# A fused attention and two-layer MLP kernel on one Trainium2 core: the first batch goes through layer 1 in single precision, and the inverse sums of the last two batches are spread by DMA

## The chip, the core and the metric

The kernel runs on one core of one Trainium2 chip. The core's engines are TensorE (PE in the profile; its weight loads are PEld), VectorE (DVE), ScalarE (ACT), GpSimd (POOL), and SyncE (SP), whose queue issues all the DMA transfers of this kernel. The metric is the device time in microseconds of one launch.

## The reference

Four batches of eight heads with 576 queries and keys of 64 features go through an attention whose scores are cut at a threshold under the row maximum. The result, 2304 rows of 512 features, goes through two MLPs with a hidden width of 2048.

```python
scores = (1 / sqrt(64)) * q @ k.T
thresh = max(scores, -1) - tau
scores = where(scores >= thresh, scores, -1e9)
attn = exp(scores - max(scores, -1));  attn = attn / (sum(attn, -1) + 1e-9)
x = (attn @ v) laid out as (2304, 512)
h = x @ w_in;   x = (s * maximum(h, 0) ** 2 + b) @ w_out           # layer 1
h = x @ w2_in;  out = (h / (1 + exp(-1.702 * h))) @ w2_out         # layer 2
```

## The kernel before

**Attention.** The heads are taken as 16 pairs, four to a batch. A pair has nine tiles of 128 queries: four of the first head, four of the second, and a ninth with the last 64 queries of both. A tile (tile_step, L425) is: scores on TensorE (L447; plain single precision, two halves of the array at once), row maximum on VectorE (nm, L456), two small VectorE instructions, exp on ScalarE (e, L474), threshold and row sum on VectorE (L478), a float16 copy on ScalarE and its rest on GpSimd (p, L487 and L488), and a DMA that transposes both (L490) into PT0, PT1 or, for the ninth tile, PTm. When a pair's nine tiles are through, finish_sums (L492) forms the inverse row sums ri. They are needed along the free axis of rs and rm; TensorE transposes a broadcast of ri (eight transposes at L525 and one at L529) and ScalarE copies the four results out. finish_main (L542) multiplies with V (mix, 28 matmuls at L550) and scales by rs in x (L561); finish_last does the same for the ninth tile from PTm (L585). Batches 0 and 1 keep x in SBUF (tiles xa and xb); batches 2 and 3 store it to DRAM (xd) and load it later.

**MLP.** Of layer 1 and layer 2, hidden (L714) makes a 128-wide slice of the hidden units from four slices of the input (L723), and project (L753) multiplies four such slices with the output weights (L779). Each operand is split in a rounded high part and the rest (split, L650; copy at L321 on VectorE or L325 on ScalarE; subtraction at L340 on VectorE or GpSimd), and each product takes three matmuls in the faster mode for 32-bit data: xa with wh, xa low with wh, xa with wl. Weights are first converted (convert, L654: three VectorE instructions at L676, L680 and L687, three ScalarE and one GpSimd, L697) and stored in DRAM (wd); for the first use they are split straight from that result (ww), later they are loaded again (wl from wd).

**Order.** All steps are put in a list and a planner (Plan.run, L120) makes the order of every engine's instructions when the program is built, from priorities (the table KN, whose t0 to t4 are due times of the passes) and costs. Each engine then executes its list in order. The passes are: layer 1 of batch 0, layer 1 of batch 1, layer 2 of both, layer 1 of batch 2, layer 1 of batch 3 with the 64-row remainders of all batches, and layer 2 of these. Attention of the next batches is woven into the passes.

Of the kernel before, what the change touches and what calls it, by code (L numbers as in the profile page):

```python
# [280 lines left out]
class Kernel:  # L281
# [9 lines left out]
    def consts(self, pool):  # L291
# [3 lines left out]
        self.identr = pool.tile([P, P], F32R, name="identr")  # L295
        nc.scalar.activation(self.identr, self.ident, AF.Copy)
# [67 lines left out]
    def prep_qk(self, p):  # L364


        nc, add = self.nc, self.plan.add
        b, hp = p["b"], p["hp"]
        k = self.at("k", [P, 2, HALF], F32, bufs=2)
        q = self.at("q", [P, 2, S], F32, bufs=2)  # L370
        p["qk"] = k, q
        self.load(lambda: k.ap, lambda: self.k[b, hp], [k], P * S * 4)
        self.load(lambda: q.ap, lambda: self.q[b, hp], [q], P * 2 * S * 4)
        add(
            {"ACT": act(S) + 93.0},
            lambda _: nc.scalar.activation(k.ap, k.ap, AF.Copy, scale=self.qs), [k], [k],
        )

    def prep_v(self, p):
# [6 lines left out]
        mx = self.at("mx", [P, 2], F32R)  # L386
# [11 lines left out]
        def spread(_):  # L398
            for h in range(2):
                nc.tensor.transpose(T[:, h].bitcast(F32R), mx[:, h : h + 1].to_broadcast([P, P]), self.identr)  # L400
# [24 lines left out]
    def tile_step(self, p, i):  # L425
# [3 lines left out]
        k, q = p["qk"]  # L429
        Sp = self.ps("S", [P, 2, 512])  # L430
        if i < 8:
            h, t = divmod(i, 4)
            PT, part = p["PT"][h], t
            cols = slice(t * P, (t + 1) * P)
            pt = lambda: PT[:, :, cols]
            heads = [(h, slice(0, P))]
        else:
            PT, part = p["PTm"], None
            cols = slice(MAIN, S)
            pt = lambda: PT.ap  # L440
            heads = [(0, slice(0, H2)), (1, slice(H2, P))]

        def scores(_):
            for h, to in heads:
                for half in range(2):
                    r = slice(half * H2, (half + 1) * H2)
                    nc.tensor.matmul(Sp[to, half, :HALF], q[r, h, cols], k[r, h, :])  # L447

        add({"PE": (pe(1, HALF, True) + 200.0, 60.0)}, scores, [k, q], [Sp])
# [42 lines left out]
    def finish_sums(self, p):  # L492
# [9 lines left out]
        if p["early"]:  # L502
# [39 lines left out]
    def finish_main(self, p):  # L542
# [16 lines left out]
        add(  # L559
            {"DVE": dve(512) + 61},  # L560
            lambda _: nc.vector.scalar_tensor_tensor(x.ap, Up.ap, vcol.ap, rs.ap, ALU.mult, ALU.mult), [Up, vcol, rs], [x],  # L561
        )
        blk, hp = self.stay.get(p["b"]), p["hp"]
        if blk:
            if "x" not in blk:
                blk["x"] = self.xtile(blk)
# [34 lines left out]
    def attention(self, pairs):  # L601
# [3 lines left out]
        for n, p in enumerate(pairs):  # L605
# [11 lines left out]
            for i in range(R):  # L617
# [7 lines left out]
                if i in (0, 4):  # L625
                    p["PT"][i // 4] = self.at(
                        "PT%d" % (i // 4), [P, R, MAIN], F16, KN["pt%d" % (i // 4)],
                        (self.xp, "xb", 1) if i else None,
# [4 lines left out]
                if i == R - 1:  # L633
                    p["PTm"] = self.at("PTm", [P, R, P], F16)
                do(lambda p: self.tile_step(p, i), p, i)
# [4 lines left out]
    def heads(self, b, start, pace, lend=False):  # L640
# [3 lines left out]
                "early": b * NP + hp < KN["early"],  # L644
# [9 lines left out]
    def convert(self, m, f, which):  # L654
# [8 lines left out]
        w, wi = lambda: wb[:, :512], lambda: wb[:, :512].bitcast(I32)  # L663
# [5 lines left out]
        def size(_):  # L669
# [20 lines left out]
            [wa, (st, 1)], [wb],  # L690
# [6 lines left out]
        add({"POOL": pool(512)}, lambda _: nc.gpsimd.tensor_tensor(wi(), wi(), low(), ALU.add), [(st, 0), wb], [wb])  # L697
        self.load(lambda: wd[:, f, :], w, [(wd, f)], P * 2048, reads=[wb])
        return wb
# [14 lines left out]
    def hidden(self, m, w, x, n):  # L714
# [4 lines left out]
        terms = [(w[i], j, kk) for kk in range(KD) for i, j in ((0, 0), (0, 1), (1, 0))]  # L719

        def mm(_, part):
            for i, (wt, j, kk) in list(enumerate(terms))[part]:
                nc.tensor.matmul(  # L723
                    hp(), wt[:, kk * P : (kk + 1) * P], x[:, j, kk, :], start=(i == 0), stop=(i == len(terms) - 1)
                )
        for h in range(2):
            part = slice(6 * h, 6 * h + 6)
            add(
                {"PE": (pe(6, n), 60.0 * h)}, lambda _, part=part: mm(_, part),
                [self.change, *w] + [(x, (t, kk)) for t in range(2) for kk in (2 * h, 2 * h + 1)], [hps],  # L730
# [22 lines left out]
    def project(self, m, c, Ws, gs, blk):  # L753
        nc, add = self.nc, self.plan.add
        n = blk["n"]
        first, last = c == 0, c == NCH - 1
# [6 lines left out]
        for i0 in range(KD if m == 0 else n // P):  # L763
            ypb = Buf(self.ph, "y", [P, 512], F32, 3)
            if m == 0:
                yp = lambda ypb=ypb: ypb[:, :n]
                acc = lambda i0=i0: accb.ap.rearrange("p (k n) -> p k n", k=KD)[:, i0, :]
                terms = [(W[i], g[j]) for W, g in zip(Ws, gs) for i, j in ((0, 0), (0, 1), (1, 0))]
# [6 lines left out]
            def mm(_, half, i0=i0, terms=terms, yp=yp):  # L775
                part = slice(i0 * P, (i0 + 1) * P)
                for i, (w, g) in list(enumerate(terms))[6 * half : 6 * half + 6]:
# [231 lines left out]
```

## Time and profile before

| | us |
|---|---|
| median of three runs | 1123.88 (1119.5, 1123.88, 1124.21) |
| the profiled execution | 1123.13 |
| its span, first to last instruction | 1121.4 |
| TensorE busy | 1045.3 |
| VectorE busy | 799.1 |
| ScalarE busy | 693.4 |
| GpSimd busy | 481.3 |

The sum of the prediction is made against the span; the profiled execution's time is 1.7 us longer than its span and 0.75 us under the median. "Busy" is the time covered by instructions of an engine. The timeline merges instructions of one kind in a row into one row with their count; of a plain single-precision matmul it holds two records. In waits, the instruction ahead of the arrow waited for the one behind it.

### The profile page before, as it was taken

To read this page: it belongs to the slowest core of one execution; us is meant where nothing else is said; L and a number is where in the kernel's file an instruction comes from. 1 tells how busy PE (TensorE), PEld (TensorE's weight loads), DVE (VectorE), ACT (ScalarE), POOL (GpSimd) and SP (SyncE) were. 2 spreads that over 40 slices of the span, in tenths; PEclk is the share of its full clock that TensorE was granted. 3 is DMA by queue.
4 is the path that set the end of the run, shared out by engine and by line. 5 is a ranking of instruction groups with operands and counts; after the bars stand their busy time and mean duration, and the time that the engine had idled before them with its cause. 6 is when DMAs were issued, how large, how long until landed. Compare 5 with 4: busy or idle time off the path is not lost.

```text
span 1121.4 us, 16483 instructions
## 1 busy us (share of the span) xinstructions
PE 1045.3 (93%) x5456; PEld 762.6 (68%) x5456; DVE 799.1 (71%) x1714; ACT 693.4 (62%) x1255; POOL 481.3 (43%) x492
## 2 busy tenths in 40 slices
PE   4667898878999999999999999999999999999998
PEld 1333565545677676776777777768888888888886
DVE  6999988899877898989987767755443644444443
ACT  5777898788788767576644677656554632323221
POOL 3767777777776668575744453510000000000000
PEclk9776898889999999999999999999999999999999
DMA  6999889797877757576754755542121211111112
GB/s 204 213 217 210 211 202 240 191 233 197 216 187 207 193 131 188 136 227 161 196 129 112 197 146 129 128 145 74 58 66 30 76 38 40 37 40 36 39 46 66
DMA packets 222597, 156.81 MB, mean 140 GB/s; under 512 B 178736, under 2 KB 179248, under 8 KB 222512
## 3 DMA queue, kind: packets, MB, share of 16 engines
q1 hardware_dynamic: 222512, 155.76, 53.5%
q8 instruction: 43, 0.70, 0.2%
q14 instruction: 42, 0.34, 0.1%
HBM read 89.13 MB, written 24.12 MB: 101 GB/s over the span
## 4 chain that ended last, share of the span: by engine, by line
PE 80%; DVE 10%; ACT 3%; issue 3%; POOL 2%; DMA 1%; SPq 0%; POOLq 0%; ACTq 0%; DVEq 0%
PE y L779 34%; PE y L723 34%; PE S L447 6%; PE T L550 3%; DVE nm L456 3%; DVE e L478 2%; PE T L525 1%; POOL ww L697 1%; POOL wl L340 1%; DVE ww L676 1%; DVE ww L687 1%; ACT e L474 1%; ACT wh L325 0%; DVE tb L461 0%; PE T L585 0%
## 5 line engine op out<-in xcount | busy, mean ns | idle before, releaser
L487 POOL TENSOR_TENSOR p<-e,p 128x512 f16<-128x512 f32 x123 | 153.4, 1247 | 131.1 <-ACT p L325 105.5
L723 PE MATMUL y<-xa,wh 128*128 128x512 f32 x512 | 169.4, 412 | 2.7 <-ACT wh L325 1.0
L723 PE MATMUL y<-xb,wh 128*128 128x512 f32 x512 | 163.8, 400 | 2.5 <-DVE xb L340 1.3
L447 PE MATMUL S<-k,q 64*128 64x288 f32 (+1 forms) x640 | 124.2, 519 | 42.7 <-DVE e L478 17.1
L340 POOL TENSOR_TENSOR gl<-gt,gh 128x512 fp32r<-128x512 f32 (+1 forms) x30 | 40.7, 1357 | 260.9 <-DVE gh L321 243.5
L474 ACT ACTIVATE e<-S,nb 128x576 f32<-128x576 f32 x144 | 104.5, 734 | 51.1 <-DVE nb L467 37.3
L456 DVE TENSOR_REDUCE nm<-S 128x1 f32<-128x576 f32 x144 | 107.1, 751 | 32.6 <-PE S L447 32.1
L779 PE MATMUL y<-gh,wh 128*128 128x512 f32 (+1 forms) x320 | 125.1, 391 | 4.7 <-DVE wh L321 3.2
L478 DVE SCALAR_TENSOR_TENSOR e<-S,tb,e 128x576 f32<-128x576 f32 x144 | 115.4, 807 | 11.2 <-ACT e L474 10.3
L779 PE MATMUL y<-gl,wh 128*128 128x512 f32 (+1 forms) x320 | 119.7, 374 | 0.0
L723 PEld LDWEIGHTS y<-xa,wh 128*128 128x128 f32 x512 | 94.6, 193 | 36.8 <-issue 8.6
L779 PE MATMUL y<-gh,wl 128*128 128x512 f32 (+1 forms) x320 | 119.5, 374 | 0.0
L744 ACT ACTIVATE gt<-y 128x512 f32<-128x512 f32 (+1 forms) x80 | 44.4, 554 | 121.4 <-PE y L723 121.2
L779 PE MATMUL y<-wh,gh 128*128 128x512 f32 x288 | 116.2, 403 | 0.0
L447 PEld LDWEIGHTS S<-k,q 64*128 64x128 f32 (+1 forms) x640 | 50.9, 203 | 96.1 <-issue 61.9
L779 PE MATMUL y<-wl,gh 128*128 128x512 f32 x288 | 114.0, 396 | 0.0
L723 PEld LDWEIGHTS y<-xb,wh 128*128 128x128 f32 x512 | 93.6, 188 | 29.8 <-issue 3.2
L779 PE MATMUL y<-wh,gl 128*128 128x512 f32 x288 | 113.9, 395 | 0.0
L747 DVE SCALAR_TENSOR_TENSOR gt<-gt,y 128x512 f32<-128x512 f32 (+1 forms) x80 | 50.5, 631 | 87.3 <-ACT gt L744 87.3
L723 PE MATMUL y<-xa,wl 128*128 128x512 f32 x256 | 103.3, 404 | 3.4 <-DVE wl L340 2.7
L340 DVE TENSOR_TENSOR gl<-gt,gh 128x512 fp32r<-128x512 f32 (+1 forms) x130 | 95.3, 749 | 15.4 <-ACT gh L325 14.6
L325 ACT ACTIVATE p<-e 128x576 f16<-128x576 f32 x123 | 83.0, 677 | 30.3 <-DVE e L478 17.4
(123 smaller groups left out, 2197.1 us busy)
## 6 DMA issues: line engine op xcount, KB each, us to landing
wl<-wd SPq DMA_DIRECT2D x128, 256.0 KB, 3.0
wst<-in_moe_w_in SPq DMA_DIRECT2D x32, 512.0 KB, 5.1
wd<-ww SPq DMA_DIRECT2D x64, 256.0 KB, 2.7
wst<-in_moe_w_out SPq DMA_DIRECT2D x32, 512.0 KB, 4.8
q<-in_q SPq DMA_DIRECT2D x16, 576.0 KB, 4.7
k<-in_k SPq DMA_DIRECT2D x16, 288.0 KB, 3.2
rv<-in_v SPq DMA_DIRECT2D x14, 320.0 KB, 3.3
xd<-rs SPq DMA_DIRECT2D x8, 256.0 KB, 2.7
```

Of the source, the lines that this page charges most:

```text
L325: nc.scalar.activation(dst(), src(), AF.Copy)
L340: engines, lambda e: self.eng[e].tensor_tensor(dst(), a(), b(), ALU.subtract), reads, writes, **kw
L447: nc.tensor.matmul(Sp[to, half, :HALF], q[r, h, cols], k[r, h, :])
L456: {"DVE": 668.0}, lambda _: nc.vector.tensor_reduce(nm.ap, Sv(), AX.XY, ALU.max, negate=True), [Sp], [nm],
L474: lambda _: nc.scalar.activation(ev(), Sv(), AF.Exp, bias=nb.ap, scale=1.0), [Sp, nb], [e],
L478: lambda _: nc.vector.scalar_tensor_tensor(ev(), Sv(), tb.ap, ev(), ALU.is_ge, ALU.mult, accum_out=p["acc"][:, i, 0:1]),
L487: nc.gpsimd.tensor_tensor(p16[:, S + H2 :], e[:, :MAIN], p16[:, :MAIN], ALU.subtract)
L550: nc.tensor.matmul(Up[h * H2 : (h + 1) * H2, :], V[:, h, slot, :], p["PT"][h][:, j, :], start=start, stop=stop)
L723: nc.tensor.matmul(hp(), wt[:, kk * P : (kk + 1) * P], x[:, j, kk, :], start=(i == 0), stop=(i == len(terms) - 1))
L744: add({"ACT": act(n, True)}, lambda _: nc.scalar.activation(t(), hp(), AF.Tanh, scale=0.851), [hps], [gt])
L747: lambda _: nc.vector.scalar_tensor_tensor(t(), t(), 1.0, hp(), ALU.add, ALU.mult), [hps, gt], [gt],
L779: nc.tensor.matmul(yp(), a, b, start=(i == 0), stop=(i == len(terms) - 1))
```

## The change

- Block 0 (batch 0 in layer 1) is marked whole. Its input x is written unsplit (xa, four slices of single precision), its weights are not split (convert writes them straight into wh), its hidden units are not split (gh is written by the ScalarE instruction that scales them), and every product is one matmul in plain single precision in place of three. Its hidden and project thus issue 64 matmuls each in place of 192. The other blocks are as before.
- For the eight pairs of batches 2 and 3 (spread: 8), finish_sums takes the path that was there but unused: one transpose of ri, one ScalarE copy to rT, a DMA of rT to DRAM (rd), and four DMAs that read it back over 64 partitions each into rs and rm.
- The tiles of a pair run in the order 0, 1, 2, 3, 8, 4, 5, 6, 7. q is laid out and loaded per head (tiles qa and qb), k as kk. The maximum over V is transposed in plain single precision (mx, no identr). A branch for scores in parts is new in the text and is taken by no pair (parts: 16).
- The table KN has t0 72.67 for 62.77, p6 3.41 for 3.17 and wq (when the next pair's q and k are loaded) 4 for 3. Lines after the change are those of the changed kernel: 788 for 723, 851 for 779, 497 for 447.

```diff
-    562.63, "t4": 650, "late": 7.58, "p5": 2.14, "p6": 3.17, "b0": 12.27, "xl": 20, "direct": 16, "c0":
+    562.63, "t4": 650, "late": 7.58, "p5": 2.14, "p6": 3.41, "b0": 12.27, "xl": 20, "direct": 16, "c0":
...
+    4, "tb": 4, "sc": 0, "eb": 3, "pb": 2, "pt0": 2, "pt1": 1, "parts": 16, "whole": 1, "raw": 1,
+    "spread": 8,
...
-        if p["early"]:
+        if p["spread"]:
             T = self.ps("T", [R, P])
             add({"PE": pe(2, P)}, lambda _: nc.tensor.transpose(T.ap, ri.ap, self.ident), [ri], [T])
...
+        to, wr = (lambda: x.ap), x
+        if blk and blk["whole"]:
+            xw = blk["x"]
+            to, wr = (lambda: xw[:, hp, :]), (xw, (0, hp))
+        add(
+            {"DVE": dve(512, psum=True) + 126},
+            lambda _: nc.vector.scalar_tensor_tensor(to(), Up.ap, vcol.ap, rs.ap, ALU.mult, ALU.mult), [Up, vcol, rs], [wr],
+        )
         if blk:
-            if "x" not in blk:
-                blk["x"] = self.xtile(blk)
+            if blk["whole"]:
+                return
...
-            for i in range(R):
+            for i, t in enumerate((0, 1, 2, 3, 8, 4, 5, 6, 7)):
...
-        terms = [(w[i], j, kk) for kk in range(KD) for i, j in ((0, 0), (0, 1), (1, 0))]
+        whole = len(w) == 1
+        pairs = ((0, 0),) if whole else ((0, 0), (0, 1), (1, 0))
+        terms = [(w[i], j, kk) for kk in range(KD) for i, j in pairs]
+        xv = (lambda j, kk: x[:, kk, :]) if whole else (lambda j, kk: x[:, j, kk, :])
...
+            g = Buf(self.gp, "gh", [P, 512], F32, self.gbufs) if whole else gt
             add(
-                {"ACT": act(n) + 93.0},
-                lambda _: nc.scalar.activation(t(), t(), AF.Identity, bias=self.b_ap, scale=self.s_ap), [gt], [gt],
+                {"ACT": act(n) + 190.0},
+                lambda _: nc.scalar.activation(g[:, :n], t(), AF.Identity, bias=self.b_ap, scale=self.s_ap), [gt], [g],
             )
+            if whole:
+                return (g,)
...
+            whole = self.passes[i][1][0]["whole"] and m == 0
+            if whole:
+                to = Buf(self.wp, "wh%d" % which, [P, 512], F32, self.wbufs[which])
...
-            self.W[i, f, which] = self.weights(m, f, which, wb)
+            self.W[i, f, which] = (to,) if whole else self.weights(m, f, which, wb)
...
-            g1 = [self.block(i, *ab[i]) for i in range(2)]
+            g1 = [self.block(i, *ab[i], whole=i < KN["whole"]) for i in range(2)]
```

On TensorE, in layer 1 of batch 0, the kernel before has the following between two score tiles (S is a tile's scores; xa the input, wh and wl a weight's two parts):

```order
L447 MATMUL S<-k,q 128x288 x4
L723 MATMUL y<-xa,wh_678 128x512 x2
L723 MATMUL y<-xa,wl_724 128x512
L723 MATMUL y<-xa,wh_678 128x512 x2
L723 MATMUL y<-xa,wl_724 128x512
L723 MATMUL y<-xa,wh_1496 128x512 x2
L723 MATMUL y<-xa,wl_1504 128x512
```

The changed kernel has there, with the second half of one slice, all of the next and the start of the first output tile (ri is the transposes of finish_sums):

```order
L788 MATMUL y<-xa,wh_1504 128x512 x2
L584 MATMUL T<-ident,ri 128x128
L497 MATMUL S<-kk,qa 128x288 x2
L788 MATMUL y<-xa,wh_497 128x512 x4
L497 MATMUL S<-kk,qa 128x288 x2
L497 MATMUL S<-kk,qa 64x288 x2
L497 MATMUL S<-kk,qb 64x288 x2
L851 MATMUL y<-gh,wh_1561 128x512
L851 MATMUL y<-gh,wh_1635 128x512
```

A slice of the hidden units was twelve matmuls and is four; a half of an output tile was six and is two.

On VectorE, at the same place (layer 1 of batch 0, beside batch 1's attention), the kernel before has:

```order
L456 TENSOR_REDUCE nm<-S 128x1
L478 SCALAR_TENSOR_TENSOR e,acc<-S,tb,e 128x576
L467 TENSOR_SCALAR nb<-nm 128x1
L461 TENSOR_SCALAR tb<-nm,under 128x1
L676 TENSOR_SCALAR ww<-wa 128x520
L340 TENSOR_TENSOR wl_1590<-ww,wh_1548 128x512
L680 TENSOR_SCALAR wa<-ww 128x65x8
L456 TENSOR_REDUCE nm<-S 128x1
L687 SCALAR_TENSOR_TENSOR ww<-wst,wa 128x512
L467 TENSOR_SCALAR nb<-nm 128x1
L461 TENSOR_SCALAR tb<-nm,under 128x1
L340 TENSOR_TENSOR gl<-gt,gh 128x512
```

and the changed kernel:

```order
L511 TENSOR_REDUCE nm<-S 128x1
L749 SCALAR_TENSOR_TENSOR wh_1635<-wst,wa 128x512
L522 TENSOR_SCALAR nb<-nm 128x1
L516 TENSOR_SCALAR tb<-nm,under 128x1
L533 SCALAR_TENSOR_TENSOR e,acc<-S,tb,e 128x576 x2
L511 TENSOR_REDUCE nm<-S 128x1
L738 TENSOR_SCALAR ww<-wa 128x520
L522 TENSOR_SCALAR nb<-nm 128x1
L516 TENSOR_SCALAR tb<-nm,under 128x1
L742 TENSOR_SCALAR wa<-ww 128x65x8
L511 TENSOR_REDUCE nm<-S 128x1
L749 SCALAR_TENSOR_TENSOR wh_1723<-wst,wa 128x512
```

The conversion of weights stays, its last VectorE instruction now writes wh itself, and the subtractions into wl and gl are gone.

On SyncE's queue, at the first pair of batch 2, the kernel before has only its usual transfers ahead of the store of x (xd):

```order
L344 DMA wl_3820<-wd_91 128x512
L344 DMA wd_93<-ww 128x512
L344 DMA wst<-in_moe_w_in 128x1024
L490 DMA_TRANSPOSE PTm<-p_3793 128x9x128
L344 DMA wl_3892<-wd_91 128x512
L490 DMA_TRANSPOSE PT_3909<-p_3885 128x9x128
L344 DMA xd_65<-rs 128x512
```

and the changed kernel:

```order
L343 DMA rd_68<-rT 9x128
L343 DMA wl_3514<-wd_89 128x512
L343 DMA rs<-rd_68 64x512 x2
L343 DMA rm<-rd_68 64x64 x2
L545 DMA_TRANSPOSE PT_3579<-p_3519 128x9x128
L545 DMA_TRANSPOSE PT_3579<-p_3534 128x9x128
L343 DMA wl_3603<-wd_89 128x512
L343 DMA xd_65<-rs 128x512
```

Five DMAs a pair are new, and the reads of rd wait in the queue until the store of rd has landed.

## Rows read from the trace of the kernel before

**Rows 1.** Stretches: us, busy PE, PEld, DVE, ACT, POOL (instructions), PEclk, DMA, GB/s

```profile
100.00:284.50 184.50, 156.48 (x820) 98.19 (x819) 166.27 (x377) 152.55 (x288) 143.04 (x144) 0.87 0.87 219
284.50:741.00 456.50, 455.73 (x2362) 323.14 (x2364) 369.37 (x775) 314.47 (x562) 268.11 (x256) 1.00 0.64 165
755.00:1121.40 366.40, 361.64 (x1836) 303.80 (x1834) 164.82 (x290) 147.43 (x270) 6.93 (x7) 1.00 0.16 49
```

**Rows 2.** Chain that ended last, by engine

```profile
PE 80%; DVE 10%; ACT 3%; issue 3%; POOL 2%; DMA 1%; SPq 0%; POOLq 0%; ACTq 0%; DVEq 0%
```

**Rows 3.** TensorE's longest wait after 284.5: us in all, times, longest

```profile
PE y L723 <- DVE xb L340: 1.3, 2, 1.0
```

**Rows 4.** Timeline of VectorE: start, us; reductions of tiles 37 and 76

```profile
99.40 0.68 DVE L676 TENSOR_SCALAR ww<-wa 128x520 f32<-128x520 f32 x1
100.03 0.76 DVE L456 TENSOR_REDUCE nm<-S 128x1 f32<-128x576 f32 x1
...
284.47 0.76 DVE L456 TENSOR_REDUCE nm<-S 128x1 f32<-128x576 f32 x1
```

**Rows 5.** VectorE's groups from 100 to 284.5: count, busy us, mean ns, idle before

```profile
L687 DVE SCALAR_TENSOR_TENSOR ww<-wst,wa 128x512 int32<-128x512 int32 x27 | 24.6, 915 | 0.0
L340 DVE TENSOR_TENSOR wl<-ww,wh 128x512 fp32r<-128x512 f32 x12 | 11.5, 959 | 2.8 <-ACT wh L325 2.8
L340 DVE TENSOR_TENSOR gl<-gt,gh 128x512 fp32r<-128x512 f32 x7 | 7.8, 1118 | 0.0
...
L561 DVE SCALAR_TENSOR_TENSOR rs<-T,vcol,rs 128x512 f32<-128x512 f32 x5 | 3.7, 748 | 3.8 <-PE T L550 3.8
L340 DVE TENSOR_TENSOR xb<-rs,xb 128x512 fp32r<-128x512 f32 x3 | 3.3, 1102 | 0.0
...
L321 DVE CAST wh<-ww 128x512 fp32r<-128x512 f32 x5 | 2.5, 492 | 1.2 <-POOL ww L697 1.2
L321 DVE CAST gh<-gt 128x512 fp32r<-128x512 f32 x2 | 1.9, 939 | 0.0
```

**Rows 6.** The same up to 100

```profile
L340 DVE TENSOR_TENSOR xa<-rs,xa 128x512 fp32r<-128x512 f32 x3 | 2.6, 870 | 0.0
```

**Rows 7.** The same from 284.5 to 741

```profile
L340 DVE TENSOR_TENSOR gl<-gt,gh 128x512 fp32r<-128x512 f32 x49 | 44.5, 930 | 1.9 <-ACT gh L325 1.6
L687 DVE SCALAR_TENSOR_TENSOR ww<-wst,wa 128x512 int32<-128x512 int32 x32 | 31.0, 972 | 0.1
```

**Rows 8.** Timeline of TensorE: two score tiles in a row, and one

```profile
51.08 2.29 PE L447 MATMUL S<-k,q 64*128 64x288 f32 x8 [2.89 <-issue]
56.05 1.33 PE L447 MATMUL S<-k,q 64*128 64x288 f32 x4 [2.67 <-DVE e L478]
```

**Rows 9.** That stretch, columns as in Rows 1

```profile
51.00:57.40 6.40, 3.64 (x13) 1.68 (x14) 6.37 (x18) 4.96 (x9) 4.87 (x6) 0.50 0.97 261
```

**Rows 10.** Timeline of TensorE where it never waits

```profile
374.56 0.39 PE L723 MATMUL y<-xb,wl 128*128 128x512 f32 x1
374.79 0.60 PE L525 MATMUL T<-ident,ri 128*64 128x128 f32 x4
375.15 0.48 PE L779 MATMUL y<-gh,wh 128*128 128x512 f32 x1
375.46 0.39 PE L779 MATMUL y<-gl,wh 128*128 128x512 f32 x1
...
380.96 3.21 PE L550 MATMUL T<-PT,V 128*64 128x512 f16 x28
384.11 0.50 PE L779 MATMUL y<-gh,wh 128*128 128x512 f32 x1
```

**Rows 11.** DMA issues from 300 to 700: count, KB, us to landing

```profile
xd<-rs SPq DMA_DIRECT2D x7, 256.0 KB, 2.8
...
xd<-xm SPq DMA_DIRECT2D x7, 32.0 KB, 2.4
```

**Rows 12.** Timeline of VectorE: the last pair's inverse sums and x

```profile
730.49 0.21 DVE L498 RECIPROCAL ri<-ri 128x9 f32<-128x9 f32 x1
...
741.43 0.75 DVE L561 SCALAR_TENSOR_TENSOR rs<-T,vcol,rs 128x512 f32<-128x512 f32 x1 [0.58 <-PE T L550]
```

More of the change, by code (lines that the diff above doesn't have):

```diff
@@ new lines, in prep_qk @@
+        if not p["parts"]:
+            k, p["q"] = part("kk"), [part("qa"), part("qb")]
+            p["k"] = k
+            self.load(lambda: k.ap, lambda: self.k[b, hp, :, :S], [k], P * S * 4)
+            for h, q in enumerate(p["q"]):
+                self.load(lambda q=q: q.ap, lambda h=h: self.q[b, hp, :, h], [q], P * S * 4)
+            add(
+                {"ACT": act(S) + 93.0},
+                lambda _: nc.scalar.activation(k.ap, k.ap, AF.Copy, scale=self.qs), [k], [k],
+            )
+            return
@@ L436, in tile_step @@
             heads = [(h, slice(0, P))]
+            at = t * P + h * (P if p["parts"] else H2)
+            qcols = [slice(at, at + P)] * 2
         else:
             PT, part = p["PTm"], None
-            cols = slice(MAIN, S)
             pt = lambda: PT.ap
             heads = [(0, slice(0, H2)), (1, slice(H2, P))]
+            n = P if p["parts"] else H2
+            qcols = [slice(MAIN, MAIN + n), slice(0, n)]
         def scores(_):
             for h, to in heads:
+                if p["parts"]:
+                    for j in range(2):
+                        for half in range(2):
+                            nc.tensor.matmul(
+                                Sp[:, half, :HALF], q[h][j][:, qcols[h]], k[h][:, half * HALF : (half + 1) * HALF],
+                                start=(h, j) == (heads[0][0], 0), stop=(h, j) == (heads[-1][0], 1),
+                            )
+                    continue
                 for half in range(2):
                     r = slice(half * H2, (half + 1) * H2)
-                    nc.tensor.matmul(Sp[to, half, :HALF], q[r, h, cols], k[r, h, :])
-        add({"PE": (pe(1, HALF, True) + 200.0, 60.0)}, scores, [k, q], [Sp])
+                    nc.tensor.matmul(Sp[to, half, :HALF], q[h][r, qcols[h]], k[r, h * HALF : (h + 1) * HALF])
+        if p["parts"]:
+            used = [t for h, _ in heads for t in (k[h], *q[h])]
+            cost = pe(4 * len(heads), HALF)
+        else:
+            used, cost = [k] + [q[h] for h, _ in heads], pe(1, HALF, True) + 370.0
+        add({"PE": (cost, 60.0)}, scores, used, [Sp])
         Sv = lambda: Sp[:, :, :HALF]
@@ L723, in mm @@
                 nc.tensor.matmul(
-                    hp(), wt[:, kk * P : (kk + 1) * P], x[:, j, kk, :], start=(i == 0), stop=(i == len(terms) - 1)
+                    hp(), wt[:, kk * P : (kk + 1) * P], xv(j, kk), start=(i == 0), stop=(i == len(terms) - 1)
                 )
         for h in range(2):
-            part = slice(6 * h, 6 * h + 6)
-            add(
-                {"PE": (pe(6, n), 60.0 * h)}, lambda _, part=part: mm(_, part),
-                [self.change, *w] + [(x, (t, kk)) for t in range(2) for kk in (2 * h, 2 * h + 1)], [hps],
+            some = len(terms) // 2
+            part = slice(some * h, some * h + some)
+            add(
+                {"PE": (pe(some, n, whole), 60.0 * h)}, lambda _, part=part: mm(_, part),
+                [self.change, *w] + [(x, (t, kk)) for t in range(1 if whole else 2) for kk in (2 * h, 2 * h + 1)], [hps],
             )
@@ L755, in project @@
         n = blk["n"]
+        whole = len(Ws[0]) == 1
+        pairs = ((0, 0),) if whole else ((0, 0), (0, 1), (1, 0))
+        some = 2 * len(pairs)
         first, last = c == 0, c == NCH - 1
@@ L767, in project @@
                 acc = lambda i0=i0: accb.ap.rearrange("p (k n) -> p k n", k=KD)[:, i0, :]
-                terms = [(W[i], g[j]) for W, g in zip(Ws, gs) for i, j in ((0, 0), (0, 1), (1, 0))]
+                terms = [(W[i], g[j]) for W, g in zip(Ws, gs) for i, j in pairs]
             else:
@@ L776, in mm @@
                 part = slice(i0 * P, (i0 + 1) * P)
-                for i, (w, g) in list(enumerate(terms))[6 * half : 6 * half + 6]:
+                for i, (w, g) in list(enumerate(terms))[some * half : some * half + some]:
                     a, b = (w[:, part], g[:, :n]) if m == 0 else (g[:, part], w.ap)
@@ L782, in project @@
                 add(
-                    {"PE": (pe(6, cols), 60.0 * half)}, lambda _, half=half, mm=mm: mm(_, half),
+                    {"PE": (pe(some, cols, whole), 60.0 * half)}, lambda _, half=half, mm=mm: mm(_, half),
                     [t for W in Ws[sel] for t in W] + [t for g in gs[sel] for t in g], [ypb],
@@ L849, in need @@
                 self.plan.prio = prio
-            self.W[i, f, which] = self.weights(m, f, which, wb)
+            elif whole:
+                wd = self.wd[m][which]
+                self.load(lambda: to.ap, lambda: wd[:, f, :], [to], P * 2048, reads=[(wd, f)])
+            self.W[i, f, which] = (to,) if whole else self.weights(m, f, which, wb)
             self.plan.prio = old
```

98 lines of the change are left out of this document (64 added, 34 removed), and 5 rows, old and new, of the table KN.

## The prediction

> **What bounds the kernel now.** I read the stretches first. The program has two halves with different limits. From 284.5 us to the end TensorE is busy 455.7 of 456.5 us and, after a short change of passes, 361.6 of 366.4 us, at the full clock (2.4 GHz) [rows 1]; its longest kind of wait there adds up to 1.3 us [rows 3]. In that half only TensorE's own work counts, and a microsecond taken off any other engine is worth nothing. The chain of waits says the same with 80% TensorE [rows 2]. From 100 to 284.5 us it is otherwise: VectorE is busy 166.3 of 184.5 us, TensorE 156.5 us at a mean granted clock of 0.87 [rows 1]. At full clock that is 156.5 x 0.87 = 136 us of work, so TensorE loses 48 us, partly idle, partly at 1.2 GHz. It is there that batch 1's attention runs beside layer 1 of batch 0, and it ends when VectorE is through with the tiles.
>
> I therefore cut the program at one instruction that both kernels have, VectorE's row maximum of tile 76 (the fourth of the ninth pair). It starts at 284.47 us [rows 4], just where TensorE's saturated half begins. The end is the time of this cut plus the TensorE work that the order leaves behind it. An earlier cut at 100.03 us, the row maximum of tile 37, is the first of batch 1 [rows 4].
>
> **What VectorE sheds ahead of the cut.** I compared the two orders up to it and priced the difference by means of this stretch. Subtractions into wl fall from 13 to 1: 12 x 0.959 = 11.5 us. All 7 into gl go: 7.8 us. One of 3 into xb moves behind the cut: 1.1 us [rows 5]. Three into xa go, ahead of tile 37: 3 x 0.870 = 2.6 us [rows 6]. Four roundings of wh go (5 to 1): 4 x 0.492 = 2.0 us; two of gh: 1.9 us. One last conversion step (0.9 us) and one x (0.7 us) move behind the cut [rows 5]. Sum 28.5 us over 31 instructions. Neighbours overlap a little: 99.40 + 0.68 ends 0.05 us after the next starts [rows 4]; 31 x 0.05 = 1.6 us, which leaves 26.9 us. All else on VectorE up to the cut is the same in number. ScalarE and GpSimd lose splits too; neither sets the pace, and I count nothing for that.
>
> Here one might expect more. Subtractions into gl take 1118 ns while GpSimd is busy 143 of 184.5 us and 930 ns later, where it is busy 268 of 456.5 us [rows 1, 5, 7]; but the conversion step, also with two inputs in SBUF, goes from 915 to 972 ns [rows 5, 7]. The Trainium skill, page "SBUF — State Buffer", section "SBUF: two separate sides", says that a VectorE operation with two SBUF inputs and a GpSimd operation exclude each other for the whole instruction. By it the fewer GpSimd subtractions would shorten the 31 conversion steps that stay; the trace agrees for gl and disagrees for the conversion. If each lost 0.1 us, the sum would be 3 us better. I take nothing.
>
> **What TensorE is left with behind the cut.** The order leaves 48 fewer split matmuls of layer 1 of batch 0, at a spacing of 0.23 us (374.56 to 374.79) [rows 10]: -11.0 us. In their place stand 14 single-precision matmuls of 512 columns. The trace has none of that shape. Two score tiles in a row take 2.29 us and one takes 1.33 us [rows 8] at a clock of 0.50 [rows 9], so a tile of 288 columns in plain single precision costs 0.96 us at 1.2 GHz, 0.48 at 2.4, and 512 columns 0.48 x 512/288 = 0.853 us. The bounds: not under three split matmuls, 0.69 us, which is what it replaces, and not over 1.33/2 x 512/288 = 1.18 us, if the fill of a lone tile came with every one. I take 0.853, from the tiles in a row, since these matmuls follow each other too. 14 x 0.853 = 11.9 us. One mix more lies behind the cut: 384.11 - 380.96 = 3.2 us [rows 10]. For eight pairs the eight transposes at L525 go; four of them take 374.79 to 375.15 and make the next matmul 0.08 us longer (0.31 for 0.23) [rows 10], 0.44 us in all: 8 x 2 x 0.44 = -7.0 us. The one transpose to rT takes the place of that at L529. Sum: -11.0 + 11.9 + 3.2 - 7.0 = -2.9 us.
>
> If VectorE went through the cut without any new wait, the span would be 1121.4 - 26.9 - 2.9 = 1091.6 us, and the execution, with the 1.7 us outside its span, 1093.
>
> **What new waiting takes back.** Layer 1 of batch 0 grows on TensorE. Between tile 37 and the cut the changed order has 114 single-precision matmuls (97.2 us) and 6 split ones (1.4 us) for 342 split ones (78.7 us), and one mix less (3.2 us): 136 + 16.7 = 153 us. The stretch shrinks from 184.4 us to 184.4 - 26.9 + 2.4 = 160 us (the 2.4 us of xa lie before it). TensorE is asked for 96% of it, against 74% now. Two engines that are both nearly full wait for each other. The least is nothing. The most is that TensorE loses the same 48 us: 153 + 48 - 160 = 41 us. Between these I went through the order from tile 37 to 73, priced by the means, and let the busier of the two engines count in each piece: over VectorE's own sum this gives 5 us for pieces of three tiles and 16 us for single tiles (0.5 and 9 us for the kernel before). Two score buffers let TensorE run ahead by about two tiles, so I take a value nearer the first: 9 us.
>
> Forecast: 1121.4 - 26.9 - 2.9 + 9 = 1100.6 us of span, 1102 us for an execution. The profiled one lies 0.75 us under the median of 1123.88, which changes nothing here.
>
> **Edits that I cost at nothing.** (1) The broadcast: rs now comes after a store to DRAM and a read, about 2.4 + 2.8 us by the nearest transfers [rows 11]. x has long to wait for its mix anyway: for the last pair 730.49 to 741.43, 10.9 us [rows 12], and the other pairs have one pair's attention between. Without that cover it would be up to 5 us at the last pair. In SyncE's queue the reads stand behind the store's landing, and behind them the next tiles' transposes and loads of wl; up to 2.4 us for each of eight pairs, if nothing is loaded ahead. (2) The ninth tile, now fifth: its transposed copy PTm has one buffer, and for five pairs its DMA must now wait for the previous pair's last mix, with later transposes behind it in the queue. Between nothing and one tile's pace (184.4/39 = 4.7 us) each, 23 us; I take nothing, as the order puts that mix within a few tiles. (3) Separate loads of q and k, the single-precision transposes of mx and the new table values: small and off TensorE's path, except the 16 x 2 transposes, at most 1-2 us.
>
> **The rivals.**
> - No new wait (1093 us). For it: the order balances the engines tile by tile. Against it: 96% leaves 7 us of slack in 160.
> - Single precision dearer. If a full-height matmul took four times the split spacing, 0.93 us, the 114 of them would add 8.8 us to a TensorE that has 7 us of slack, and the 14 behind the cut 1 us: 1112 us. For it: the split matmul itself takes 0.23 us where 512 columns at 2.4 GHz are 0.213. Against it: the score tiles.
> - The broadcast in the queue: eight pairs each hold the weights' loads up by 2.4 us, and TensorE stops for all of it: 1102 + 19 = 1121 us, no change. Against it: TensorE waits next to nothing in that half [rows 3].
> - Slower: TensorE becomes the bound of the early stretch with its present losses. It drops to 1.2 GHz after each wait for a late tile, where a single-precision matmul is 1.7 us, and the 48 us stay. The cut then comes 41 us later than without waits: 1093 + 41 = 1134 us. It decides from a loss of 30 us over the waitless case on. For it: clock 0.87 now; against it: more of TensorE's work is on hand, so there is less to wait for.
>
> **How the numbers follow.** The forecast has 0.60, no new wait 0.14, dearer matmuls 0.12, the queue 0.08, slower 0.06. What a measurement can tell from no change is about 0.5%, 5.6 us: 1118.3 to 1129.5 us. The first three are faster: 0.86; the queue is the same: 0.08; the last slower: 0.06. The range runs from 1091 us (the waitless case and a little of the shorter VectorE steps) to 1118 us (dearer matmuls with some of the ninth tile's wait); it leaves out the queue and the slower case and a little below. The forecast alone has 1096 to 1110 us.
>
> **What will show it.** The fourth tile of the ninth pair should start its row maximum near 284.5 - 27 + 9 = 267 us; TensorE should be saturated from there on, with no new wait in the pairs of batches 2 and 3. In the stretch of layer 1 of batch 0 its granted clock should rise above 0.87 and its busy share above 0.9, with VectorE still near 0.9. A single-precision matmul should start every 0.85 us in a row. I am wrong if the cut comes no earlier, if matmuls of layer 1 wait for VectorE as long as now, or if TensorE shows waits behind rs or wl after the cut.

## The result and the profile after

The changed kernel takes 1104.85 us (median of 4 runs, 1104.03 to 1105.94) beside 1123.27 us for the kernel before: ratio 0.984 (95%: 0.982 to 0.987). Timed again it had 0.984 (0.982 to 0.986); there one execution of six took 2028.86 us, and the median of the other five, 1102.62 us, is the one used below. The forecast was 1102 us, range 1091 to 1118, faster. The profiled execution has a span of 1103.9 us.

The stretches of the changed kernel, cut at the same two row maxima (columns as in [rows 1], which they answer):

```profile
101.20:267.30 166.10, 157.80 (x687) 68.79 (x688) 147.34 (x352) 131.61 (x246) 100.98 (x114) 0.98 0.92 230
267.30:723.40 456.10, 453.30 (x2339) 316.62 (x2337) 380.80 (x790) 302.75 (x536) 266.59 (x258) 1.00 0.70 176
737.40:1103.90 366.50, 361.79 (x1837) 303.92 (x1835) 164.09 (x290) 146.58 (x269) 5.73 (x6) 1.00 0.16 49
```

The two saturated stretches last what they lasted (456.1 and 366.5 us for 456.5 and 366.4). The whole gain lies in the first: 166.1 us for 184.5. In it TensorE went from 156.5 busy us at a clock of 0.87 to 157.8 at 0.98, so it now does 154.7 us of full-clock work where it did 136; VectorE went from 166.3 busy us to 147.3.

VectorE's timeline at the two marks (start, us), which answers [rows 4]:

```profile
101.22 0.75 DVE L511 TENSOR_REDUCE nm<-S 128x1 f32<-128x576 f32 x1
...
267.33 0.75 DVE L511 TENSOR_REDUCE nm<-S 128x1 f32<-128x576 f32 x1
```

Tile 37 comes 1.2 us later than before, tile 76 (the cut) 17.1 us earlier. Behind the cut the kernel before took 836.9 us and this one takes 836.6.

The chain of waits by engine, beside [rows 2]. In this profile it can be followed back only to 204 us, so its shares (73% TensorE, 4% VectorE) add up to 81% and say nothing of the stretch. In a second profile of the same kernel it reaches the start:

```profile
PE 82%; DVE 11%; ACT 3%; DMA 2%; issue 2%; POOL 0%; SPq 0%; ACTq 0%; POOLq 0%; DVEq 0%
```

VectorE's share of the chain is what it was (11% for 10%). VectorE's groups from 101.2 to 267.3 us, against [rows 5]:

```profile
L749 DVE SCALAR_TENSOR_TENSOR wh<-wst,wa 128x512 int32<-128x512 int32 x27 | 25.2, 938 | 0.6 <-PE y L788 0.6
...
L457 DVE SCALAR_TENSOR_TENSOR V<-rv,vs,V 128x320 f16<-128x320 f32 x8 | 6.4, 814 | 0.1
...
L623 DVE SCALAR_TENSOR_TENSOR rs<-T,vcol,rs 128x512 f32<-128x512 f32 x3 | 2.2, 745 | 0.2 <-PE T L605 0.2
L339 DVE TENSOR_TENSOR xb<-rs,xb 128x512 fp32r<-128x512 f32 x2 | 1.7, 863 | 0.0
...
L339 DVE TENSOR_TENSOR wl<-wl,wh 128x512 fp32r<-128x512 f32 x1 | 0.7, 680 | 0.0
```

In the kernel before, the line of V's low half (V) was

```profile
L419 DVE SCALAR_TENSOR_TENSOR V<-rv,vs,V 128x320 f16<-128x320 f32 x8 | 4.6, 605 | 0.2 <-ACT V L327 0.2
```

The subtractions into gl are gone, and of those into wl one is left, as the order said. The single-precision matmuls run in blocks. Of TensorE's timeline (each matmul leaves two records, so x4 is two and x8 is four matmuls):

```profile
204.75 1.88 PE L788 MATMUL y<-xa,wh 128*128 128x512 f32 x4
206.47 1.88 PE L851 MATMUL y<-gh,wh 128*128 128x512 f32 x4
208.28 0.76 PE L497 MATMUL S<-kk,qb 64*128 64x288 f32 x4
208.96 1.98 PE L851 MATMUL y<-gh,wh 128*128 128x512 f32 x4
210.88 0.76 PE L497 MATMUL S<-kk,qa 64*128 64x288 f32 x4
211.56 3.70 PE L788 MATMUL y<-xa,wh 128*128 128x512 f32 x8
215.10 3.60 PE L851 MATMUL y<-gh,wh 128*128 128x512 f32 x8
```

Read the starts, not the lengths. From 204.75 to 206.47 are 1.72 us for two, 0.86 us each. Two that stand between score tiles take longer, 208.96 to 210.88, 0.96 us each. 211.56 to 215.10 is 3.54 us for four, 0.885 us each.

TensorE's waits from the cut to the end (us in all, times, longest), against [rows 3]:

```profile
PE S L497 <- DVE e L533: 2.5, 2, 1.8
PE y L788 <- ACT xb L324: 1.9, 1, 1.9
PE y L788 <- DVE xb L339: 0.9, 1, 0.9
```

No wait of TensorE stands behind rs or a load of wl. For the last pair, VectorE's timeline beside [rows 12]:

```profile
710.83 0.21 DVE L553 RECIPROCAL ri<-ri 128x9 f32<-128x9 f32 x1
721.21 0.75 DVE L623 SCALAR_TENSOR_TENSOR rs<-T,vcol,rs 128x512 f32<-128x512 f32 x1
```

and the reads of the broadcast from 300 to 700 us, with the time to landing, beside [rows 11]:

```profile
rs<-rd SPq DMA_DIRECT2D x14, 128.0 KB, 2.9
```

From ri to x there are 10.4 us. The last pair's reads are issued by 715.0 us and land some 3 us later, at 718; x starts at 721.2. The trip is covered with 3 us to spare.

### The profile page after: what moved, and what is told of

The parts are those of the page before. It is cut to its first block, busy times and chain, and to the rows that moved or that the text cites. A ratio compares the mean times of both kernels' runs of the same rounds, so it can differ in the third digit from the quotient of the medians.

```text
span 1103.9 us, 16038 instructions
## 1 busy us (share of the span) xinstructions
PE 1044.2 (95%) x5264; PEld 727.7 (66%) x5264; DVE 787.2 (71%) x1696; ACT 654.5 (59%) x1176; POOL 430.5 (39%) x460
## 4 chain that ended last, share of the span: by engine, by line
PE 73%; DVE 4%; DMA 2%; ACT 1%; issue 1%; POOL 0%; SPq 0%; POOLq 0%; DVEq 0%; ACTq 0%
PE y L851 34%; PE y L788 33%; PE S L497 4%; PE T L605 2%; DMA PTm<-p 1%; DVE nm L511 1%; DMA wst<-in_moe_w_in 1%; DVE e L533 1%; DMA wst<-in_moe_w_out 0%; DVE wh L749 0%; DMA wl<-wd 0%; PE T L646 0%; DVE ww L738 0%; DVE wl L339 0%; ACT e L529 0%
## 5 line engine op out<-in xcount | busy, mean ns | idle before, releaser
L542 POOL TENSOR_TENSOR p<-e,p 128x512 f16<-128x512 f32 x123 | 150.6, 1224 | 141.2 <-ACT p L324 123.8
L788 PE MATMUL y<-xa,wh 128*128 128x512 f32 x512 | 184.5, 453 | 2.5 <-POOL wh L759 2.5
L851 PE MATMUL y<-gh,wh 128*128 128x512 f32 (+1 forms) x384 | 157.2, 453 | 0.0
L339 POOL TENSOR_TENSOR gl<-gt,gh 128x512 fp32r<-128x512 f32 (+1 forms) x16 | 20.6, 1291 | 227.1 <-DVE gh L320 221.5
L788 PE MATMUL y<-xb,wl 128*128 128x512 f32 x256 | 101.5, 397 | 0.0
L339 DVE TENSOR_TENSOR gl<-gt,gh 128x512 fp32r<-128x512 f32 (+1 forms) x128 | 88.3, 705 | 14.8 <-ACT gh L324 13.8
L851 PEld LDWEIGHTS y<-gh,wh 128*128 128x128 f32 x384 | 71.3, 189 | 41.4 <-issue 28.2
L851 PE MATMUL y<-gl,wh 128*128 128x512 f32 (+1 forms) x256 | 94.3, 368 | 0.0
L851 PE MATMUL y<-gh,wl 128*128 128x512 f32 (+1 forms) x256 | 94.2, 368 | 0.0
L497 PE MATMUL S<-kk,qa 64*128 64x288 f32 (+1 forms) x320 | 67.1, 509 | 28.1 <-DVE e L533 15.9
```

The source lines that it names most:

```text
L339: engines, lambda e: self.eng[e].tensor_tensor(dst(), a(), b(), ALU.subtract), reads, writes, **kw
L497: nc.tensor.matmul(Sp[to, half, :HALF], q[h][r, qcols[h]], k[r, h * HALF : (h + 1) * HALF])
L542: nc.gpsimd.tensor_tensor(p16[:, S + H2 :], e[:, :MAIN], p16[:, :MAIN], ALU.subtract)
L788: nc.tensor.matmul(hp(), wt[:, kk * P : (kk + 1) * P], xv(j, kk), start=(i == 0), stop=(i == len(terms) - 1))
L851: nc.tensor.matmul(yp(), a, b, start=(i == 0), stop=(i == len(terms) - 1))
```

## The experiments

Each kernel is the changed one with the edit shown. Ratios are to the kernel before, run beside it. "The cut" is the row maximum of tile 76; "the stretch" runs from tile 37 to it; "the remainder" is what comes after the cut. When the table or the order of tiles is edited, the planner makes a new order of instructions. By the traces TensorE, VectorE, ScalarE and GpSimd keep the changed kernel's order, but for what is added or left out, in the four runs that edit single steps (a quarter of the matmuls left out, the masking step doubled or left out, two PTm buffers). With the transposes for all pairs they keep it up to 308 us, with batch 1 whole up to 150 us; in the other runs they leave it within the first 60 us.

**Which part carries the gain.** First, batch 0's layer 1 split again:

```
-    ... "parts": 16, "whole": 1, "raw": 1,
+    ... "parts": 16, "whole": 0, "raw": 1,
```

> The changed kernel with batch 0's layer 1 split again in three matmuls (whole 0), all else kept (broadcasts, order of the tiles, table). Theory A, VectorE's relief ahead of the cut carries the gain: the terms of it, -26.9 on VectorE, +4.1 of TensorE work behind the cut and +9 of waits, go, so 1104.9 + 13.8 = 1119 us, and the row maximum of tile 76 is back near 284 us. Rival B, the gain is the new order of the tiles and the table, not the missing splits: at most 1108 us.

1123.11 us, ratio 1.002 (1.000 to 1.003). The cut came at 288.3 us. The gain is gone, so the rival falls; 4 us more went than the ledger had. The loss lies in two places: tile 37 came at 106.9 us, 5.7 later than in the changed kernel and 6.9 later than in the kernel before, and the stretch took 181.4 us, 15.2 more than in the changed kernel. The remainder was 835.6 us.

Second, the inverse sums of the last eight pairs by transposes again:

```
-    "spread": 8,
+    "spread": 16,
```

> The changed kernel with the inverse sums of all pairs spread by TensorE and ScalarE again (spread 16). Theory A: eight pairs get 0.88 us each of transposes back in the half where TensorE never waits, 1104.9 + 7 = 1112 us. Rival: the stores, reads and waits in SyncE's queue had eaten that, 1105 us or less.

1114.27 us, ratio 0.993 (0.992 to 0.995), where the changed kernel has 0.984: the broadcast is worth about 10 us. The stretches from the cut to the end, first the changed kernel's:

```profile
267.30:1103.90 836.60, 826.59 (x4211) 629.43 (x4209) 552.93 (x1093) 456.44 (x817) 274.87 (x266) 1.00 0.45 120
```

and the one with transposes:

```profile
266.60:1111.90 845.30, 834.35 (x4276) 636.39 (x4274) 551.68 (x1091) 469.90 (x843) 277.57 (x266) 1.00 0.44 116
```

The cut stays (the order up to it is the same) and TensorE has 7.8 us more to do behind it. The ledger had 7.0.

Third, the ninth tile last again:

```
-            for i, t in enumerate((0, 1, 2, 3, 8, 4, 5, 6, 7)):
+            for i, t in enumerate((0, 1, 2, 3, 4, 5, 6, 7, 8)):
```

> The changed kernel with the tiles of a pair in the old order, the ninth last. Theory A: the tile order is worth nothing measurable, 1105 us within 3. Rival: the 3.6 us that the changed kernel is late at tile 37 against the forecast come from the ninth tile's early place, whose transposed copy has to wait for the previous pair's last mix: 1101 us, tile 37 near 97.5 us in place of 101.2.

1108.14 us, ratio 0.988 (0.987 to 0.990). Its two marks:

```profile
97.63 0.75 DVE L511 TENSOR_REDUCE nm<-S 128x1 f32<-128x576 f32 x1
...
264.35 0.76 DVE L511 TENSOR_REDUCE nm<-S 128x1 f32<-128x576 f32 x1
```

The rival had the place right: tile 37 comes 3.6 us earlier, and the cut 3.0. But the remainder took 842.0 us, 5.4 more, and the kernel is 3.3 us slower. Neither expectation had that: Theory A had no measurable change, the rival a gain.

Fourth, batch 1's layer 1 in single precision as well:

```
-    ... "parts": 16, "whole": 1, "raw": 1,
+    ... "parts": 16, "whole": 2, "raw": 1,
```

> The changed kernel with batch 1 whole in layer 1 too (whole 2). Theory A: layer 1 of batch 1 lies behind the cut, where only TensorE's work counts; 128 matmuls of 0.853 us for 384 of 0.23 to 0.234 us are +20 us, less whatever of them the order still puts ahead of the cut: 1120 to 1125 us, slower than the changed kernel. Rival: the relief of VectorE and ScalarE helps wherever it is given, 1105 us or less.

1139.2 us, ratio 1.015 (1.013 to 1.017): slower, and by more than Theory A had. The stretch:

```profile
101.44:278.59 177.15, 167.95 (x701) 71.54 (x701) 151.01 (x360) 132.32 (x248) 98.00 (x111) 0.96 0.90 232
```

TensorE has 10.1 us more in it than in the changed kernel, and the stretch is 11.0 us longer. The remainder grew by another 23.1 us, of which TensorE's busy time is 16.3.

The three parts taken back one by one cost 20, 10 and 4 to 5 us by their ratios; together they were worth 18. With split weights the other two parts and the new table win nothing: what the stretch is shorter there than before the change (3.1 us) is less than what is lost ahead of tile 37 (6.9 us). Which edit loses it is open; the table's start times went with the single-precision batch, and no run has it by itself.

**What bounds the stretch now.** TensorE is busy 95% of it. So I took work from TensorE alone; each of the two loops skips the fourth term:

```
+                    if whole and i == 3:
+                        continue
...
-        ... stop=(i == len(terms) - 1)
+        ... stop=(i == len(terms) - 1 - whole)
```

> The changed kernel, but of every four single-precision matmuls that add up to one tile of batch 0's layer 1 the fourth is left out, so that a quarter of each of these sums is missing; all else and its order stay. It takes about 114 x 0.25 x 0.86 = 24 us of TensorE's work out of the stretch before the cut (the row maximum of tile 76) and 3 us out of what lies behind. Theory A (VectorE's own work paces the stretch; only waits that come of TensorE being nearly full can go): the cut comes at most the 9 us of forecast waits earlier, 258 to 262 us, and the time is 1104.9 - 7 - 3 = about 1095 us. Rival (TensorE's work is what the stretch now lasts): the cut comes 24 us earlier, at 243, and the time is about 1078 us. Second rival (VectorE alone, no coupling): the cut stays at 267, 1102 us.

1103.29 us, ratio 0.985 (0.983 to 0.987). The stretch, then TensorE's two longest kinds of wait from 97 to 265 us:

```profile
101.23:268.01 166.78, 142.43 (x629) 60.54 (x630) 146.34 (x353) 131.05 (x246) 99.97 (x114) 0.92 0.90 230
```

```profile
PE S L497 <- DVE e L533: 9.2, 10, 1.4
PE T L580 <- DVE ri L553: 8.3, 5, 2.5
```

TensorE is busy 15.4 us less and at a lower clock (142.4 x 0.92 = 131 us of full-clock work for 154.7), and the cut did not move; TensorE only waits longer for VectorE. Theory A and the first rival fall, the second rival holds: in the changed kernel the amount of TensorE's work costs VectorE nothing that this run can show.

Then VectorE alone: one step of the weights' conversion done twice, or left out.

```
-            lambda _: tsc(
+            lambda _: [tsc(
                 a().bitcast(I32), flat().bitcast(I32), 3, 0x3FFFFFF8, ALU.logical_shift_left, ALU.bitwise_and
-            ),
+            ) for _ in range(2 if to is not wb else 1)],
```

> The changed kernel in which VectorE does the masking step of the weights' conversion (L742, wa from ww) twice over for the weights of batch 0's layer 1; the second writes the same values. The order of all other instructions stays. It adds 6 instructions of 0.68 us before tile 37 and 26 in the stretch up to the cut, 32 x 0.5 to 0.68 = 16 to 22 us of VectorE's time, somewhat less where neighbours overlap. Theory A, new after the run with a quarter of the single-precision matmuls left out (the cut did not move when TensorE got 15 us of slack): VectorE's own work with a constant 18 us of waits for other engines sets the stretch. The cut then comes 14 to 20 us later, 281 to 287 us, and the time goes back to about 1118 to 1124 us. Rival (the 18.8 us in which VectorE is idle there take it up): cut 267 to 272, time under 1110 us.

1116.28 us, ratio 0.995 (0.993 to 0.997), 13.7 us over the changed kernel's 1102.62 beside it (12 us by the ratios). The stretch:

```profile
104.86:278.98 174.12, 161.71 (x689) 69.52 (x689) 160.55 (x376) 132.34 (x246) 100.21 (x114) 0.96 0.90 221
```

13.2 us more of VectorE's work in the stretch lengthen it by 8.0; another 3.6 us come ahead of tile 37. The rest comes out of VectorE's waits, which fall from 18.8 to 13.6 us. The cut, at 279.0, came 11.7 us later in place of 14 to 20. So the size is two thirds of what Theory A gave, but VectorE does pace it, and the rival falls. With `range(0 if to is not wb else 1)` the step is left out:

> The changed kernel in which the masking step of the weights' conversion (L742) is left out for the weights of batch 0's layer 1, so that these weights are wrong; the order of all other instructions stays. VectorE loses 6 instructions before tile 37 and 26 in the stretch, 16 to 22 us. Theory A (VectorE paces the stretch until TensorE's own work does): TensorE has 158 us of work in the 166 us from tile 37 to the cut, so it becomes the bound after some 8 us; with 2 to 3 us won ahead of tile 37 the cut comes 8 to 11 us earlier, 256 to 259 us, and the time is 1094 to 1097 us. Rival (TensorE's share counts for nothing here either): the cut comes 16 us earlier or more, 251 us, 1089 us. Second rival (VectorE's sum does not pace the stretch): cut 267, 1105 us.

1102.78 us, ratio 0.982 (0.980 to 0.985): the same as the changed kernel's 1102.62 and 0.984 beside it. The stretch, and VectorE's longest waits in it:

```profile
100.61:263.74 163.13, 156.09 (x684) 68.04 (x685) 133.84 (x326) 130.83 (x244) 100.46 (x113) 0.98 0.93 233
```

```profile
DVE e L533 <- ACT e L529: 9.5, 14, 1.6
DVE nm L511 <- PE S L497: 6.9, 8, 1.6
```

VectorE lost 13.5 us of work and the stretch 3.0 us; 10.5 us turned into waits. All three expectations missed the size; nearest is that VectorE's sum no longer counts. Side by side, in us:

| stretch from tile 37 to the cut | VectorE busy | TensorE busy | length | VectorE idle |
|---|---|---|---|---|
| before | 166.2 | 156.4 | 184.4 | 18.2 |
| changed | 147.3 | 157.8 | 166.1 | 18.8 |
| TensorE less | 146.3 | 142.4 | 166.8 | 20.4 |
| VectorE more | 160.6 | 161.7 | 174.1 | 13.6 |
| VectorE less | 133.8 | 156.1 | 163.1 | 29.3 |
| batch 1 whole too | 151.0 | 168.0 | 177.2 | 26.1 |

The changed kernel stands near a corner. More work on VectorE lengthens the stretch (13.2 us give 8.0). So did the run with 10.1 us more on TensorE (11.0), but it had 3.7 us more on VectorE and another order as well. Less on one engine alone gives 0 or 3. VectorE's longest kinds of wait in the changed kernel's stretch show that what holds it there is not TensorE alone:

```profile
DVE e L533 <- ACT e L529: 5.8, 12, 1.0
DVE ww L738 <- ACT wa L733: 5.2, 7, 2.9
DVE nm L511 <- PE S L497: 2.9, 2, 1.6
DVE xa L623 <- PE T L605: 2.4, 1, 2.4
```

Of the 18.8 us, 11.0 end on ScalarE and 6.1 on TensorE; of the 10.5 us that came with VectorE's relief, 4.8 and 4.4. The chain of the second profile, which reaches through the stretch, also goes through two loads of weights there:

```profile
166.32 6.35 DMA wst<-in_moe_w_in
258.86 5.27 DMA wst<-in_moe_w_out
```

That relief of VectorE and TensorE together would shorten the stretch is an inference: no run relieved both, and none relieved ScalarE or the DMAs by themselves, so either may be the next to hold it.

**The ninth tile and the early part.** A second buffer for its transposed copy:

```
-                    p["PTm"] = self.at("PTm", [P, R, P], F16)
+                    p["PTm"] = self.at("PTm", [P, R, P], F16, 2)
```

> The changed kernel with two buffers in place of one for PTm, the transposed copy of the ninth tile, which is now worked on fifth. The order of TensorE's instructions stays the same. Theory A (my step that costs the one buffer at nothing): 1104.9 us within 2. Rival (each pair's ninth transposed copy waits for the last mix of the pair before, with later transposes behind it in SyncE's queue; at the most 23 us in my bound, and the place of the 3 us that the old order of tiles won ahead of tile 37): 1100 us or less, with tile 37 near 98 us.

1104.65 us, ratio 0.985 (0.983 to 0.987), tile 37 at 100.3 us: Theory A, no more. The one buffer costs nothing that can be measured.

The broadcast for all pairs (`"spread": 0`):

> The changed kernel with the inverse sums spread by the trip through DRAM for all 16 pairs and not for the last 8 alone. Behind the cut nothing changes (836.6 us). Ahead of it TensorE loses 16 transposes for each of some 8 pairs, 0.44 us for four at full clock, 7 us there, about half of it in the stretch of layer 1 of batch 0, and ScalarE or VectorE two copies of 512 columns for each pair. Theory A (VectorE paces the stretch and TensorE's share there only through waits): the cut comes 1 to 4 us earlier and the time is 1101 to 1104 us. Rival (the early pairs have no cover for the trip through DRAM, which stands in SyncE's queue with the loads of q, k and the transposes): the cut comes later, 1108 us or more.

1109.57 us, ratio 0.990 (0.988 to 0.992): slower, the rival's sign. Tile 37 came at 97.0 us but the cut at 269.0; the stretch grew by 5.9 us although TensorE had less to do. VectorE waited 11.1 us there for ScalarE's exponents, against 5.8; what delayed them, the queue or the order, I did not separate.

Last, the ninth tile last in the first nine pairs and fifth in the other seven:

```
-            for i, t in enumerate((0, 1, 2, 3, 8, 4, 5, 6, 7)):
+            for i, t in enumerate(range(R) if n < 9 else (0, 1, 2, 3, 8, 4, 5, 6, 7)):
```

> The changed kernel with the ninth tile last in the first nine pairs, as before the change, and fifth in the other seven, as after it. Two parts were seen together when the ninth tile was put last everywhere: the cut came 2.9 us earlier and what lies behind it took 5.4 us longer. If these two are effects of separate places, as I hold, this kernel keeps the first and not the second: cut near 264.5, remainder near 837, 1102 us. Rival (the remainder's 5.4 us are work that the earlier cut only pushed behind it): remainder 840 or more and 1105 us or over.

1104.2 us, ratio 0.985 (0.983 to 0.987), its marks at 97.5 and 264.1 us, the remainder 837.1. By the marks Theory A; by the time no gain. So both kernels were timed again, side by side:

> The changed kernel as it is, beside the kernel with the ninth tile last in the first nine pairs (below), on the same chip and with the same runs of the kernel before. 1103 to 1105 us.

> The kernel with the ninth tile last in the first nine pairs and fifth in the other seven, against the changed kernel in the same call. Its one profile had the cut 3.2 us earlier and the remainder 0.5 us longer. Theory A (this gain is real): 2 to 3 us under the changed kernel. Rival (the next runs take it up, as its first median of 1104.2 says): within 1 us of it.

1102.62 us for the changed kernel, 1106.34 for the mixed one (ratios 0.984, 0.982 to 0.986, and 0.985, 0.983 to 0.987). The second profile of the mixed kernel has its marks at 99.2 and 267.5 us: the gain of 3 us was one profile's. By the ratios the two can't be told apart, and none of the versions beats the changed kernel. The new place of the ninth tile may pay in the last seven pairs: last everywhere 0.988 (0.987 to 0.990), last in the first nine 0.985 (0.983 to 0.987, both times). The intervals touch, so that is likely and not shown.

## Why the prediction was right

**The cut: 267 us forecast, 267.3 measured, by three misses that cancel.** The mechanism held: VectorE's work ahead of the cut paces the kernel there, as the run with the masking step doubled shows. That the size fits to a microsecond is luck.
- VectorE sheds less than I counted. Of 26.9 us, 24.5 lay in the stretch; its busy time there fell by 18.9. The step that failed is the overlap of neighbours: I took 0.05 us for each instruction that goes, from one pair of rows. The durations of the VectorE instructions that start in the stretch add up to 191.0 us before and 168.7 after, the busy time to 166.2 and 147.3; of 22.3 us of durations, 3.4 had been overlap, over twice my 1.4. Most of the rest of the 5.6 us: the instructions that stay were taken at their old price, but V's low half went from 605 ns to 814 (1.7 us for 8) and the conversion step from 915 to 938 (0.6 us for 27), and the small steps of one tile more (0.7 us) fall into the stretch.
- The new waits did not come. I gave 9 us for two engines that are both nearly full; VectorE's idle time went from 18.2 to 18.8. The run with 15.4 us less on TensorE won none of the 18.8 us back. Waits do come when VectorE gets another 13.5 us less: they take back 10.5. But only 4.4 us of these end on TensorE and 4.8 on ScalarE, so two full engines waiting for each other are at most a part of it.
- Tile 37 was forecast at 97.6 us and came at 101.2. I had looked at the early part only for the three subtractions that go. With the ninth tile last it came at 97.6, 97.5 and 99.2 us, with it fifth and the changed kernel's order up to there at 101.2, 100.3, 99.8, 99.5 and 101.2. So the new order of tiles costs some 2 us there, little more than such a mark varies; the step that held it for free looked only at the copy's buffer, and that one is indeed free.

In sum 5.6 - 8.4 + 3.6 = 0.8 us.

**Behind the cut** TensorE's busy time fell from 829.6 us (of 836.9) to 826.6: the ledger's -2.9 us, measured as -3.0. The fit to 0.1 us is luck too: four more profiles with the same order of TensorE's instructions have between 824.2 and 828.4 us. That only 0.3 us of it shows in this profile (a second one of the same kernel has 833.7 us) is 2.7 us more of short waits. The broadcast's share was right too, and larger than it looks in the ledger: without it the ledger would have stood at +4.

**The single-precision matmul** was 0.86 us in a row for my 0.853, up to 0.96 beside score tiles, and TensorE's work in the stretch 154.7 us for my 153. The rival with dearer matmuls (0.93 us, 8.8 us more) falls with this sum, which came out only 1.7 us above the forecast. The queue rival falls by the waits behind the cut, and the slower one by the clock: 0.98 in the stretch, and TensorE did not keep its 48 us of losses but 11.4 (166.1 - 154.7).

**The signs I named.** The cut, the clock, TensorE's share (95%) and VectorE's (89%) came as written; "no new wait" in the later batches was nearly so, two kinds of 2.5 and 1.9 us. "No new wait at all" was the better account of the stretch, but its 1093 us rested on the same shed that was too large.

**The place where rule and row were weighed.** I set the conversion step's mean against GpSimd's busy share, and that reading was wrong. The share fell from 78% to 61% and the mean grew from 915 to 938 ns, but single instructions show what the means hide:

```profile
191.17 0.69 DVE L749 SCALAR_TENSOR_TENSOR wh<-wst,wa 128x512 int32<-128x512 int32 x1
...
193.54 1.16 POOL L542 TENSOR_TENSOR p<-e,p 128x512 f16<-128x512 f32 x1 [0.15 <-POOL wh L759]
193.76 1.47 DVE L749 SCALAR_TENSOR_TENSOR wh<-wst,wa 128x512 int32<-128x512 int32 x1
...
194.65 0.75 POOL L543 TENSOR_TENSOR p<-e,p 128x64 f16<-128x64 f32 x1
```

Without a GpSimd instruction beside it the step takes 0.69 us, with one 1.47. In the whole trace of the changed kernel the 20 steps with GpSimd busy for less than a twentieth of their time took 674 to 693 ns, and the 24 with GpSimd busy throughout 1129 ns in the mean; in the kernel before, 13 took 670 to 689 ns and 29 took 1109. V's low half behaves alike (539 to 553 ns and 1085). The masking step, with one SBUF input, stayed under 0.70 us either way. So the trace agrees, for the conversion step too, with the rule of the Trainium skill, page "SBUF — State Buffer", section "SBUF: two separate sides", that such a VectorE instruction and a GpSimd instruction exclude each other. What counts is how many of the steps the order puts beside GpSimd's instructions: of 27 in the stretch it was 21 before and 20 after, so nothing was won; of the 8 for V's low half it was 3 and 5, with which go the 1.7 us above. Taking nothing came out right for another reason than mine.

## What to carry to other kernels

Price a shed instruction by what it takes from the engine's busy time, not by its own duration: compare the sum of durations with the busy time of the stretch first. Here 13% of the durations was overlap, and of the durations shed 15%. In a stretch with two engines at 95% and 89%, less work on either one alone won little (15.4 us on TensorE nothing, 13.5 us on VectorE 3), while more work on VectorE cost 60% of its size. Before a mean is set against another engine's busy share, compare single instructions with and without that engine beside them. When a forecast comes out to the microsecond, check its terms one by one: here three were off by 4 to 8 us.

## What was not expected of the hardware

The early part does not run alike in executions of one program. The changed kernel's first hundred us, in its two profiles:

```profile
0.00:50.00 50.00, 23.77 (x147) 12.18 (x149) 39.81 (x119) 31.85 (x55) 23.24 (x38) 0.82 0.87 209
50.00:100.00 50.00, 35.34 (x219) 17.01 (x215) 45.97 (x134) 34.03 (x60) 30.95 (x44) 0.63 0.93 202
```

```profile
0.00:50.00 50.00, 26.28 (x145) 12.97 (x145) 39.42 (x119) 31.30 (x54) 22.61 (x38) 0.94 0.86 207
50.00:100.00 50.00, 32.11 (x226) 16.23 (x224) 47.83 (x137) 35.33 (x62) 32.23 (x45) 0.77 0.95 207
```

The granted clock was 0.82 and 0.63 in the one, 0.94 and 0.77 in the other, tile 37 came at 101.2 and 99.8 us, and the spans were 1103.9 and 1100.2 us. Over the profiles that share the changed kernel's order up to the cut, tile 37 came between 99.5 and 101.2 us while the stretch from there to the cut was steadier, 166.0 to 167.1; over the five that share TensorE's whole order the remainder was 833.7 to 839.6. So a mark of a single profile is good to about 2 us here and a remainder to 6; what I read of the tile order from single profiles was hardly larger.
